# Fused FFT convolution and gated feed-forward: first filter spectrum from partial sums, short convolution on two halves of the array's rows, three weight groups kept from block to block, and a new order

## The chip, the cores and the metric

The kernel runs on one core of one Trainium2 chip. The metric is the device time of one execution in microseconds (us). A core has five engines that run side by side: PE (TensorE, matrix products; its weight loads are listed as PEld), DVE (VectorE), ACT (ScalarE), POOL (GpSimd) and SP (SyncE, which here only issues DMAs). PE writes into PSUM; ACT or DVE must copy ("evict") what it wrote to SBUF before the bank can be used again.

## The reference

All data are bfloat16, the sequence has S = 2048 steps and D = 640 channels, the feed-forward is F = 1728 wide.

```python
x = A_q
k_shift = sum over t in 0..3 of k_pad[:, t:t+S, :] * shift_k[:, 3 - t]      # causal, 4 taps per channel
kv = k_shift * v
y = irfft(rfft(kv, zero-padded to 2S) * rfft(ssm_k, zero-padded to 2S))[:S] # long causal convolution per channel
y = y + kv * ssm_D
h = x + layernorm(x) * y
out = h + (silu(layernorm(h) @ w_gate) * (layernorm(h) @ w_up)) @ w_down
```

## The kernel before

The sequence is worked in four blocks j of 512 steps. A block is a tile of 128 partitions with R = 4 rows (r) of 640 channels each.

For every block, g (the filter `ssm_k`) is turned by PE transposes or by DMA (`g_turned`, L453). k goes through the 4-tap short convolution and is multiplied by v (`kv_of`, L621). `spectrum` and `transform` (L506, L369) turn g into G[j] and kv into X[j] by matrix products with a fixed cosine and sine basis WF (the helper `forward`, L375). The outputs come as two halves, "low" and "high", each with four rows of 640. By the rule "sub" the even rows r are summed first (evicted, times two), then the odd ones are added, and DVE takes the difference (L410). By `DIRECT`, which the first filter block G0 alone uses, the second half comes instead from two more products per group with a second basis, `minus` (L1205 loads it): 6 products of 320 columns where "sub" needs 4.

`window` joins two blocks' filter spectra to H. `mac` (L707) forms the products X[i]·H[j-i] and sums them into A on DVE: a term is a product (L746) and a sum (L747). The inverse (L813, matrix products L878 with WI), two layer norms (`norm`, L760, on DVE or POOL) and a turn of the result (`turn_h`) give hT. Some sums are handed to the DMA engines, which add into memory (`add_into`, L276); these are issued by POOL.

`ffn` (L966 on) takes block j - 1 while block j is transformed: seven weight groups of gate and up columns, each loaded by two (the last by four) DMAs (`load_w`, L959), 27 times 5 products of 512 columns (L1022), then 112 products of 320 columns (or as many columns cut otherwise) with w_down (L1110). All seven groups are loaded again in each of the four blocks. Only blocks 0 to 2 have a transform of another block beside them; the last block's feed-forward stands alone at the end.

The short convolution of block 0 (`mm`, L639) uses, for each r, 5 channel groups times 4 taps = 20 products of 128 columns: the stationary operand is a 128 by 128 piece of turned k, the moving one a diagonal matrix of that tap's weights (`diag`, filled at L1166). In blocks 1 to 3 (`mm2`, L648) two taps share one product: the tile T holds k twice, the second copy one step later on the other 64 partitions, so that a product over 128 partitions does two taps for 64 channels, with 64 columns; 20 products again. The copies inside T are made by DMA (L563) and by ACT (L565, `TCOPY`), and `pairs` is a second table of tap weights (L1185, on POOL, from a second turn of the taps at L1175).

The order of all work is written out by hand, not found at build time: each piece of work is an `Op` with a number, and `ORDER` lists these numbers. An entry -n takes the piece's second form (`op.other`, another engine or queue). Every engine runs its own pieces in the order of the list and waits, in order, for what they need. Tiles named big, S, row, ps and so on are buffers out of pools (12 big, 8 S, 5 row, 4 ps); which one a piece gets follows from `ORDER` too.

```python
op = self.ops[n if n >= 0 else ~n]
...
if n < 0:
    op.eng, op.ns, op.fn = op.other
```

The first lines of the program keep PE busy with products of ones (`spin`, L1151, 18, 16 and 16 of them).

Of the kernel before, what the change touches and what calls it, by code (L numbers as in the profile page):

```python
# [31 lines left out]
ADDLO = ('G1', 'G2', 'X1', 'X2', 'X3')  # L32
ADDMAC = ()
ADDWIN = (1,)
ADDH = (1, 2)
LEAD = {}
PAD = 16
DIRECT = ('G0',)
ACTLN = 0
ACTKV = 0  # L40
ACTLN2 = (0, 1, 2, 3)
LN1DVE = ()
LN2POOL = (1, 2)
HTURN = (1, 3, 2)
GTURN = (3,)
KTURN = (1, 2, 3)
SUM = {'X3': 'four', 'i2': 'four', 'i3': 'four', 'G3': 'four'}
ADDP = {(1, 1): ((0, 1),)}
ADDINV = (2,)
WHOLE3 = False  # L50
WARMUP = (18, 16, 16)
MERGE = ()
WIDE = ()
H1ACT = ()
PAIRED = True
K0TURN = False
EARLY = True
FFN4 = True
KVPAIR = ()
DPOOL = False  # L60
LASTCUT = 2
DIAGDVE = 4
ATURN = ()
GLOAD = (1, 2, 3, 'T')
FIRST = False
TWOTAPS = True
TWONS = 640
TCOPY = (1, 2)
# [43 lines left out]
HALVES = (ROWS[:2], ROWS[2:])  # L112


def make_basis():

# [96 lines left out]
def kernel(ctx: ExitStack, tc: tile.TileContext, A_q, A_k, A_v, A_shift_k, A_ssm_k, A_ssm_D, B_x,  # L213
# [369 lines left out]
    def load_k(j):  # L583
        if TWOTAPS and j:
            return load_two(j)
# [745 lines left out]
```

## Time and profile before

| | |
|---|---|
| time, median of 3 runs (lowest to highest) | 261.48 us (260.77 to 261.54) |
| the profiled execution's own time: span, first to last instruction | 259.6 us |
| PE busy | 251.3 us (97%) |
| DVE busy | 198.6 us (77%) |
| ACT busy | 180.0 us (69%) |
| POOL busy | 97.0 us (37%) |
| moved by DMA | 45.38 MB |
| granted TensorE clock | 1.000 |

The profiled execution has only its span; the runs' median lies 1.9 us above it. "Busy" of PE counts a product from its start to its modelled end, and products overlap, so PE's rate is read from the spacing of a run of products, not from its busy time. A line number is a line of the kernel before; in the kernel after the same statement has another number, and the table of the change gives those that matter.

### The profile page before, as it was taken

What the parts mean: (1) busy time and instruction counts of PE and PEld (TensorE: products, weight loads), DVE (VectorE), ACT (ScalarE), POOL (GpSimd) and SP (SyncE); (2) the same over time, 40 slices, a digit from 0 to 9 for tenths busy, and PEclk for the clock granted to TensorE, in tenths of its full rate; (3) what the DMA queues carried; (4) which work ended last, traced back from release to release, by engine and by line L of the source; (5) the groups of instructions that cost most, each with busy time, mean ns of one, the idle gap of its engine ahead of it and who ended that gap; (6) DMA issues with size and microseconds to landing.
All of it is one profiled execution on the core that took longest, in us unless ns stands there. A gap on an engine that the chain in (4) does not pass through costs nothing.

```text
span 259.6 us, 4700 instructions
## 1 busy us (share of the span) xinstructions
PE 251.3 (97%) x1803; PEld 154.2 (59%) x1818; DVE 198.6 (77%) x259; ACT 180.0 (69%) x297; POOL 97.0 (37%) x115
## 2 busy tenths in 40 slices
PE   8999899999998999999999999999999999999994
PEld 7967577654654477754465477544456764444663
DVE  4679999999998999999999999999998200004403
ACT  2899999999998998569855985655497134637200
POOL 7961300008914199926117962240951022000000
PEclk9999999999999999999999999999999999999999
DMA  6997999979999998999997965994498546000002
GB/s 218 403 251 119 289 252 340 280 115 279 247 238 168 182 217 204 190 191 201 214 231 110 299 151 107 198 238 130 100 215 255 101 77 70 8 0 0 13 15 76
DMA packets 64752, 45.38 MB, mean 175 GB/s; under 512 B 31014, under 2 KB 60267, under 8 KB 64731
## 3 DMA queue, kind: packets, MB, share of 16 engines
q1 hardware_dynamic: 58896, 32.96, 51.1%
q0 software_dynamic: 5824, 12.13, 24.9%
q8 instruction: 14, 0.23, 0.4%
q14 instruction: 8, 0.06, 0.1%
q10 hardware_dynamic: 10, 0.01, 0.0%
HBM read 30.01 MB, written 4.59 MB: 133 GB/s over the span
## 4 chain that ended last, share of the span: by engine, by line
PE 78%; ACT 9%; DMA 6%; DVE 2%; issue 2%; SPq 1%; ACTq 0%; DVEq 0%
PE ps L1022 40%; PE ps L1110 23%; PE ps L375 10%; DMA big<-in_B_w_up_dram 4%; PE ps L878 3%; DMA big<-in_A_q_dram 3%; ACT T L565 2%; ACT big L364 1%; ACT S L364 1%; PE ps L648 1%; ACT row L757 1%; ACT big L664 1%; ACT big L473 1%; ACT tT L1014 1%; DVE row L892 1%
## 5 line engine op out<-in xcount | busy, mean ns | idle before, releaser
L1022 PE MATMUL ps<-big,big 128*128 128x512 bf16 x525 | 119.9, 379 | 1.7 <-DMA big<-in_B_w_up_dram 0.8
L1022 PEld LDWEIGHTS <-big 128*128 128x128 bf16 x540 | 52.5, 98 | 61.1 <-DMA big<-in_B_w_up_dram 1.3
L1110 PE MATMUL ps<-wd,tT 128*128 128x320 bf16 (+1 forms) x416 | 60.3, 299 | 0.0
L1110 PEld LDWEIGHTS <-tT 128*128 128x128 bf16 x416 | 40.7, 98 | 16.3
L1016 DVE TENSOR_TENSOR tT<-tT,co 128x2048 bf16<-128x2048 bf16 x12 | 14.5, 1219 | 34.4 <-ACT tT L1014 32.4
L375 PE MATMUL ps<-big,WF 128*128 128x320 bf16 x240 | 39.1, 299 | 1.3 <-ACT big L364 1.0
L1012 ACT CAST co<-ps 128x1024 bf16<-128x1024 f32 x24 | 24.2, 1011 | 17.3 <-PE ps L1022 16.8
L747 DVE TENSOR_TENSOR S<-S,big 128x2560 bf16<-128x2560 bf16 x23 | 34.3, 1492 | 1.2 <-DMA S<-big 0.5
L746 DVE TENSOR_TENSOR big<-S,S 128x2560 bf16<-128x2560 bf16 x23 | 34.1, 1485 | 0.2
L375 PEld LDWEIGHTS <-WF 128*128 128x128 bf16 x240 | 23.1, 97 | 12.8 <-issue 2.3
L1014 ACT ACTIVATE tT<-ps 128x1024 bf16<-128x1024 f32 x24 | 24.5, 1029 | 8.8 <-PE ps L1022 8.7
L757 ACT ACTIVATE row<-big 128x640 bf16<-128x640 bf16 x32 | 23.5, 742 | 1.8 <-DMA big<-in_A_q_dram 1.1
L807 ACT ACTIVATE row<-big,sm 128x640 bf16<-128x640 bf16 x23 | 20.3, 922 | 3.8 <-POOL sm L789 2.8
L1117 POOL DMA_DIRECT2D out_dram<-row x12 | 11.8, 1010 | 29.2 <-ACT row L1116 29.1
L364 ACT CAST S<-ps 128x320 bf16<-128x320 f32 (+1 forms) x36 | 19.4, 583 | 0.3
L1116 ACT CAST row<-ps 128x640 bf16<-128x640 f32 x12 | 8.1, 691 | 14.2 <-PE ps L1110 13.2
L364 ACT ACTIVATE big<-ps 128x640 bf16<-128x640 f32 (+1 forms) x24 | 15.6, 696 | 0.7 <-PE ps L375 0.7
L278 POOL DMA_DIRECT2D big<-row x8 | 7.0, 919 | 22.9 <-DVE row L892 22.9
L892 DVE SCALAR_TENSOR_TENSOR row<-row,ps 128x640 bf16<-128x640 bf16 x16 | 12.8, 815 | 1.1 <-PE ps L878 0.9
L278 POOL DMA_DIRECT2D S<-big x2 | 2.5, 1266 | 26.3 <-DVE S L719 19.1
L719 DVE TENSOR_TENSOR big<-S,S 128x2560 bf16<-128x2560 bf16 (+1 forms) x10 | 12.2, 1218 | 0.1
L959 POOL DMA_DIRECT2D big<-in_B_w_gate_dram x8 | 9.1, 1137 | 8.1 <-PE ps L1022 7.8
(110 smaller groups left out, 330.4 us busy)
## 6 DMA issues: line engine op xcount, KB each, us to landing
big<-in_B_w_up_dram SPq DMA_DIRECT2D x17, 320.0 KB, 5.1
big<-in_B_w_gate_dram SPq DMA_DIRECT2D x16, 320.0 KB, 4.7
big<-in_A_ssm_k_dram SPq DMA_DIRECT2D x4, 640.0 KB, 9.2
big<-in_A_q_dram SPq DMA_DIRECT2D x4, 640.0 KB, 7.6
big<-in_A_v_dram SPq DMA_DIRECT2D x4, 640.0 KB, 6.9
big<-in_B_w_gate_dram POOLq DMA_DIRECT2D x8, 320.0 KB, 7.2
big<-in_B_w_up_dram POOLq DMA_DIRECT2D x7, 320.0 KB, 6.7
wd<-in_B_w_down_dram SPq DMA_DIRECT2D x1, 2080.0 KB, 12.2
```

What stands on the lines that cost most here:

```text
L364: (lambda: nc.scalar.activation(dst(), src(), ACT.Copy, scale=2.0)) if twice else (lambda: nc.scalar.copy(dst(), src())),
L375: nc.tensor.matmul(ap(ps)[:, h, 0:NH], w, ap(src)[:, r, h * NH:(h + 1) * NH], start=(first and i == 0), stop=(last and i == len(rs) - 1), ...
L746: nc.vector.tensor_mul(flat2(b), X.part(xs), H.part(hs))
L747: f(A.part(dst), A.part(dst), flat2(b))
L757: act(825, lambda r=r, junk=junk: nc.scalar.activation(ap(junk), ap(x)[:, r, :], ACT.Square, scale=D ** -0.5, accum_out=sm(s, 1)[:, r:r + ...
L807: nc.scalar.activation(ap(row), ap(x)[:, r, :], ACT.Identity, bias=sm(s, 5)[:, r:r + 1], scale=sm(s, 4)[:, r:r + 1])
L892: nc.vector.scalar_tensor_tensor(two(ap(t)), two(ap(t)), 1.0, half(ap(ps)), op0=ALU.mult, op1=ALU.mult, accum_out=sm(s, 0)[:, r:r + 1])
L1012: act(1010, lambda ps=ps: nc.scalar.copy(ap(co)[:, at:at + 2, :], ap(ps)), src, [(co, gi % 2)])
L1014: act(1010, lambda ps=ps: nc.scalar.activation(ap(tT)[:, c:c + 2, :], ap(ps), ACT.Silu), src, [done(range(c, c + 2), ROWS)])
L1016: dve(1220, lambda: nc.vector.tensor_mul(ap(tT)[:, c - 2:c + 2, :], ap(tT)[:, c - 2:c + 2, :], ap(co)), [co], [done(range(c - 2, c + 2), R ...
L1022: nc.tensor.matmul(ap(ps)[:, i, :], ap(w)[:, k, off:off + P], ap(hT)[:, k, :], start=(k == 0), stop=(k == KT - 1))
L1110: nc.tensor.matmul(ap(ps)[:, hf, to:to + n], t, ap(wd)[:, c, col + (hf - hs[0]) * NH:col + (hf - hs[0]) * NH + n], start=(c == order[0]), ...
```

## The change

It has five parts, made together.

1. G0 comes by "sub" like the other blocks (`DIRECT` is empty): 32 products of 320 columns in place of 48, the `minus` basis is not loaded, and DVE takes two differences of half width more.
2. The short convolution of every block uses one table `diag` (128 by 64 for a channel group and tap) and one copy of k. A product runs over 64 partitions, the lower or the upper half of the array's rows, with 64 columns; for each r there are 5 groups times 4 taps times 2 halves = 40 products, alternating between the halves, and the halves write to two PSUM banks. The second copy of k in T, `pairs`, the second turn of the taps and all copies inside T go. A small tile `halo` keeps the last three steps of block 0.
3. `load_w` keeps the last three weight groups of a block for the next one (`KEEP`), and every second block takes the groups in reversed order, so that the kept ones come first.
4. Every sum that may be made by DVE or by a DMA is now one helper (`sum_into`), and the choice is made by the sign in `ORDER`; likewise the layer norms (POOL or DVE). On DVE 17 of the sums at L622 (before L747: 23) are left; the DMA makes 10 sums of 640 KB (before 4) and 6 of 160 KB (before 8). Four norms run on DVE (before two).
5. `ORDER` is new throughout, and the third `spin` is gone.

| what | line before | line after |
|---|---|---|
| transform products | L375 | L353 |
| short convolution | L639, L648 | L577 |
| tap table | L1166, L1185 | L965 |
| inverse products | L878 | L748 |
| gate and up, down | L1022, L1110 | L852, L906 |
| product, sum of a term | L746, L747 | L619, L622 |
| weight loads | L959 | L810 |

```diff
-DIRECT = ('G0',)
+DIRECT = ()
-WARMUP = (18, 16, 16)
+WARMUP = (18, 16)
-GLOAD = (1, 2, 3, 'T')
+GLOAD = (0, 1, 2, 3)
+KEEP = (3, 3, 3)
-    0, 2, 31, 1, 4, 5, 7, 10, 6, 8, 16, 13, 12, 11, 22, 29, 26, 37, 27, 14, 3, 15, 23, 28, 42, -39, 9, 35, -37, 24, 39, 205, 40,
+    4, 0, 21, 2, 14, 1, 3, 5, 20, 7, 6, 46, 18, -48, 48, 50, 8, 51, 52, 24, -54, 19, 22, 49, -14, 30, -26, 54, 28, 26, 31,
...
+GROUPS = (0, 1, 2, 3, 4, 5, 6)
...
-    def add_into(to, what, r, w, n=R * D):
+    def sum_into(ns, fn, to, what, r, w, n=R * D, dma=False):
+        def by_dma():
+            nc.gpsimd.dma_start(out=to(), in_=what(), accum_op=ALU.add, max_dma_last_dim=2 * D * 2)
+        a, b = ("dve", ns, fn), ("add", 958.0 if n == D else 3830.0, by_dma)
...
+    T = fixed([P, KT * TW], BF16, "T")
+    halo = fixed([P, KT, 3], BF16, "halo")
+    diag = fixed([P, KT, 4, H2], BF16, "diag")
...
-            def mm(r=r, ps=ps):
+            def mm(r=r, out=out):
                 for c in range(KT):
                     for t in range(4):
-                        q, off = (r - t, PAD) if r >= t else (r - t + 4, PAD - 1)
-                        k = tk0()[:, c, q, off - PAD + 1:off - PAD + 1 + P] if TWOTAPS else ap(kT)[:, c, q, off:off + P]
-                        nc.tensor.matmul(line(ap(ps))[:, c * P:(c + 1) * P], k,
-                                         ap(diag)[:, 4 * c + t, :], start=(t == 0), stop=(t == 3))
+                        for b in range(2):
+                            at = slice(b * H2, (b + 1) * H2)
+                            if j:
+                                k = tk()[at, c, PAD + r - t:PAD + r - t + 4 * P - 3:4]
+                            else:
+                                q, off = (r - t, 1) if r >= t else (r - t + 4, 0)
+                                k = tk0()[at, c, q, off:off + P]
+                            nc.tensor.matmul(out()[:, b, c, :], k, ap(diag)[at, c, t, :], start=(t == 0), stop=(t == 3))
...
-            def mm2(r=r, ps=ps):
-                for c in range(KT):
-                    for b in range(2):
-                        lo = c * P + b * H2
-                        for p in range(2):
-                            at = PAD + r - 2 * p
-                            nc.tensor.matmul(line(ap(ps))[:, lo:lo + H2], tk()[:, b, c, at:at + 4 * P - 3:4],
-                                             ap(pairs)[:, 4 * c + 2 * b + p, :], start=(p == 0), stop=(p == 1))
...
     def load_w(gi):
+        if gi in kept:
+            return kept[gi]
...
+        kept[gi] = w
+        return w
...
+        order = GROUPS if j % 2 == 0 else GROUPS[::-1]
+        for n, gi in enumerate(order):
...
+            if j == NB - 1 or n < NGRP - KEEP[j]:
+                kept.pop(gi)
```

How the order moves, at three places. First SP's queue at the start: the loads of block 0 (ssm_k is g, q is x). Before:

```order
L597 DMA T<-in_A_k_dram 128x2560
L330 DMA big_73<-in_A_ssm_k_dram 128x5x512
L342 DMA big_74<-in_A_q_dram 128x2560
L337 DMA big_75<-in_A_v_dram 128x2560
L1199 DMA WF<-const_wf 128x2048
L342 DMA big_76<-in_A_q_dram 128x2560
L1205 DMA tT_84<-const_minus 128x2048
```

and now:

```order
L308 DMA big_72<-in_A_ssm_k_dram 128x5x512
L514 DMA big_73<-in_A_k_dram 128x2560
L977 DMA WF<-const_wf 128x2048
L320 DMA big_75<-in_A_q_dram 128x2560
L315 DMA big_76<-in_A_v_dram 128x2560
L308 DMA big_79<-in_A_ssm_k_dram 128x5x512
```

The filter and the basis WF moved ahead of k and of x and v; `minus` is gone.

Second, POOL at the start, where the tap table is filled. Before, `big_72` holds diag (DVE fills the other 16 pieces):

```order
L1180 TENSOR_TENSOR row_87<-ident 128x64
L1170 COPY row_87<-row_86 5x512
L1166 TENSOR_SCALAR big_72<-ident,taps 128x128 x4
L1188 MEMSET root 128x4
L1189 MEMSET tail 64x512
L1185 TENSOR_SCALAR pairs<-row_87,taps_107 128x64 x12
```

and now:

```order
L960 TENSOR_TENSOR row_86<-ident 128x64
L986 DMA row_87<-in_A_ssm_D_dram 1x16x40
L965 TENSOR_SCALAR diag<-row_86,taps 128x64 x8
L547 COPY halo<-T 128x15
L965 TENSOR_SCALAR diag<-row_86,taps 128x64 x4
L969 MEMSET root 128x4
```

POOL now fills 12 of the 20 pieces that the first convolution reads, and the last four stand behind a copy that reads all of block 0's turned k.

Third, POOL a little later, while block 1 is transformed: the sums that DMAs make (S is a spectrum, `sm` the small tile of a layer norm). Before:

```order
L554 COPY T<-T 64x10x3
L278 DMA S_71<-big_75 128x2x1280
L775 TENSOR_TENSOR sm_98<-sm_98 128x4
L785 TENSOR_TENSOR sm_98<-sm_98 128x4
L786 TENSOR_SCALAR sm_98<-sm_98 128x4
L787 TENSOR_TENSOR sm_98<-sm_98,root 128x4
L789 TENSOR_TENSOR sm_98<-sm_98 128x4
L278 DMA S_67<-S_69 128x2x1280
```

and now:

```order
L255 DMA S_67<-S_68 128x2x1280
L255 DMA S_71<-big_72 128x2x1280
L653 TENSOR_TENSOR sm_99<-sm_99 128x4
L663 TENSOR_TENSOR sm_99<-sm_99 128x4
L664 TENSOR_SCALAR sm_99<-sm_99 128x4
L665 TENSOR_TENSOR sm_99<-sm_99,root 128x4
L666 TENSOR_TENSOR sm_99<-sm_99 128x4
L255 DMA S_71<-S_71 128x2x1280
```

Before, these were two of the four sums of 640 KB in the whole queue; now they are the first three of ten, and a window sum stands ahead of the norm.

More of the change, by code (lines that the diff above doesn't have):

```diff
@@ L600, in turned_k @@
     def turned_k(k, behind=None, table=None):
-        if plan.block in KTURN or not plan.block and K0TURN:
+        if plan.block:
             return k
-        src = rd if plan.block else plain
-        kT = T if TWOTAPS else new("kT")
         for r in range(R):
@@ L614, in turned_k @@
             evict(lambda copy, r=r, pt=pt: copy(
-                tk0()[:, :, r, 1:] if TWOTAPS else ap(kT)[:, :, r, PAD:], turned(pt)[:, 0:D].rearrange("p (c t) -> p c t", c=KT)),
-                [pt], [of_t(("K", r)) if TWOTAPS else (kT, r)], other=490)
+                tk0()[:, :, r, 1:], turned(pt)[:, 0:D].rearrange("p (c t) -> p c t", c=KT)), [pt], [of_t(("K", r))], other=490)
             if table:
                 plan.ops[-1].deps.add(table)
-        return kT
-    def kv_of(j, kT, before, v, behind=None):
-        two_taps = TWOTAPS and j > 0
-        if j == 0:
-            dve(60, lambda: nc.vector.memset(tk0()[:, :, :, 0:1] if TWOTAPS else ap(kT)[:, :, :, PAD - 1:PAD], 0.0), [],
-                [of_t("K0") if TWOTAPS else (kT, "halo")])
-        elif not two_taps:
-            plan.add("pool", 900, lambda: nc.gpsimd.tensor_copy(ap(kT)[:, :, :, PAD - 1:PAD], ap(before)[:, :, :, PAD + P - 1:]),
-                     [(before, r) for r in range(R)], [(kT, "halo")])
+        firsts.append(plan.add("pool", 500, lambda: nc.gpsimd.tensor_copy(ap(halo), tk0()[:, :, 1:R, P]), [of_t(*FIRSTS)], [halo], (),
+                               ("act", 240, lambda: nc.scalar.copy(ap(halo), tk0()[:, :, 1:R, P]))))
@@ L630, in kv_of, with by_half, out @@
+        return T
+    firsts = []
+    def kv_of(j, v, behind=None):
+        if j == 0:
+            dve(60, lambda: nc.vector.memset(tk0()[:, :, :, 0:1], 0.0), [], [of_t("K0")])
         kv = new("t4")
-        for r in (0, 2, 1, 3) if plan.block in KVPAIR else range(R):
+        def by_half(t):
+            return t.rearrange("p (c b x) -> p b c x", c=KT, b=2)
+        for r in range(R):
             ps = conv_ps()
-            def mm(r=r, ps=ps):
+            def out(ps=ps):
+                return half(ap(ps)).rearrange("p b (c x) -> p b c x", c=KT)
+            def mm(r=r, out=out):
@@ L707, in mac, with straight @@
-    def mac(A, X, H, first, pieces=((0, 1),), adds=(), at=None):
-        if at in MERGE:
-            merged(A, X, H, first, [a for a in adds if isinstance(a, int)])
-            return
-        adds = [a for a in adds if not isinstance(a, int)]
+            if j == 0:
+                firsts.append(op)
+            def straight(r=r, out=out):
+                nc.vector.tensor_mul(by_half(ap(kv)[:, r, :]), out(), by_half(rd(v)[:, r, :]))
+            op = plan.add("act", 700, lambda r=r, out=out: nc.scalar.copy(by_half(ap(kv)[:, r, :]), out()), [ps, v], [(kv, r)], (), ("dve", 820, straight))
@@ L714, in mac @@
+            op.rest = dve(490, lambda r=r: nc.vector.tensor_mul(ap(kv)[:, r, :], ap(kv)[:, r, :], rd(v)[:, r, :]), [v], [(kv, r)])
+        return kv
+    def mac(A, X, H, first, pieces=((0, 1),)):
         for ws in pieces if first else ():
@@ L961, in load_w, with ffn @@
         plan.name = was
-        return (w, 0), (w, 2 * P)
-    paired = []
-    def ffn(j, hT, h, end=False, lead=0):
+        kept[gi] = w
+        return w
+    kept = {}
+    def ffn(j, hT, h, end=False):
         tT = new("tT")
@@ L1080, in ffn @@
-        first, then = ROWS[:2], ROWS[2:]
-        for gi in range(0, lead, 2):
-            chunks((gi, gi + 1), first)
-        for gi in range(lead, NGRP - 1):
-            by_four(gi) if FFN4 else chunks((gi,), ROWS)
-        behind = odd_by_four() if FFN4 else odd_chunks()
-        for gi in range(0, lead, 2):
-            behind = chunks((gi, gi + 1), then)
+        order = GROUPS if j % 2 == 0 else GROUPS[::-1]
+        for n, gi in enumerate(order):
+            if gi == NGRP - 1:
+                last = odd_by_four()
+            else:
+                close = gi // 2 in [g // 2 for g in order[:n]]
+                if not close:
+                    co = new("co")
+                last = by_four(gi, co, close)
+            if j == NB - 1 or n < NGRP - KEEP[j]:
+                kept.pop(gi)
@@ L1088, in ffn @@
+        behind = last
         for r in ROWS:
             ps = new("ps_f")
-            order = list(range(lead * 2, NCH)) + list(range(lead * 2))
+            order = list(range(NCH))
             last = end and r == ROWS[-1]
@@ L1190 @@
     plan.add("pool", 600, lambda: nc.gpsimd.memset(ap(wd)[64:P, NC_FULL, :], 0.0), [ident], [(wd, "zero")])
-    turns = [op for op in plan.ops if op.eng in ("turn", "aturn")]
     first("Lx0")
     x = load_x(0)
-    if FIRST:
-        plan.ops[-1].then.update(turns)
     first("Lv0")
@@ L1202 @@
     first("Lm")
-    minus = new("tT")
+    minus = new("tT") if DIRECT else None
     if DIRECT:
@@ L1212 @@
     first("k0")
-    k = turned_k(k, spun, table)
-    again = spun
-    if not K0TURN:
-        again = spin(WARMUP[2])
-        again.deps.update(op for op in plan.ops if op.name == "k0" and op.eng == "pe" and op is not again)
-    kv = kv_of(0, k, None, v, again)
+    turned_k(k, spun, table)
+    kv = kv_of(0, v)
     first("g0")
@@ L1229 @@
     A = Spec(new("S"))
-    at = len(plan.ops)
     mac(A, X[0], H[0], True, split("m"))
-    plan.ops[at].then.update(fills)
     first("i0")
-    s = inverse(A, x, n1, split("i"), minus if "inv0" in DIRECT else None, HALVES if LEAD.get(0) else (ROWS,))
+    s = inverse(A, x, n1, split("i"), minus if "inv0" in DIRECT else None, (ROWS,))
     first("t0")
@@ L1248 @@
         stage("Lk")
-        before, k = k, load_k(j)
+        load_k(j)
         stage("Lv")
```

402 lines of the change are left out of this document (91 added, 311 removed), and 72 rows, old and new, of the table ORDER.

## The prediction

> **What bounds the kernel now.** I read the page's busy times first, then the busy time by stretch, then the chain of waits, and last the timelines of the places that the change touches. The page's first row says that PE is busy almost throughout; the table by stretch (PE, DVE and ACT, each with its time and its count of instructions) says where each engine is.
>
> ```profile
> PE 251.3 (97%) x1803; PEld 154.2 (59%) x1818; DVE 198.6 (77%) x259; ACT 180.0 (69%) x297; POOL 97.0 (37%) x115
> ...
> 12.80:28.00 15.20, 14.57 (x116) 10.10 (x114) 13.31 (x24) 14.83 (x42) 5.85 (x14) 1.00 0.97 196
> 28.00:50.00 22.00, 20.50 (x223) 15.02 (x222) 21.55 (x44) 21.49 (x40) 2.44 (x4) 1.00 1.11 286
> 50.00:82.00 32.00, 30.90 (x225) 16.80 (x228) 31.42 (x31) 30.78 (x42) 14.46 (x12) 1.00 0.99 225
> 82.00:197.00 115.00, 114.58 (x723) 66.30 (x730) 112.59 (x108) 85.46 (x136) 59.62 (x56) 1.00 0.88 189
> 212.00:256.00 44.00, 43.90 (x243) 23.82 (x244) 7.28 (x9) 15.92 (x19) 2.58 (x3) 1.00 0.13 21
> ```
>
> Up to 197 us two engines are full at once, PE and DVE (112.59 of 115 us); after 212 us PE is alone. PE busy can hide a slow stream, so I check its rate in the chain of waits (start, length, what).
>
> ```profile
> 97.53 2.72 PE ps L1110 x20
> ...
> 114.09 10.74 PE ps L1022 x49
> ...
> 130.01 0.66 PE ps L648 x20
> ...
> 189.99 0.54 PE ps L878 x4
> ```
>
> A product of 320 columns takes 2.72/20 = 136 ns, one of 512 columns 219 ns, one of 64 columns 33 ns; from 81 us to the end the chain is PE products one behind the other. So PE's count of products times these spacings is the span, plus the head, the tail and the gaps. The gaps behind the head are small: 0.63 + 1.50 + 1.10 us in the first three stretches, 0.42 us in the fourth. DVE nevertheless sets PE at one late place, the inverse of block 3:
>
> ```profile
> 186.62 1.49 DVE L826 TENSOR_TENSOR S<-S 128x2560 bf16<-128x2560 bf16 x1
> 188.14 1.56 DVE L843 TENSOR_TENSOR S<-S 128x1280 bf16<-128x1280 bf16 x2
> ```
>
> L843 ends at 189.70 us and its reader L878 starts at 189.99 us. A saving on PE ahead of that place needs a saving on DVE as well, or other work for PE to do meanwhile.
>
> **First G.** 48 products become 32; 16 fewer at 136 ns are **-2.2 us** on PE, all on the path, since the stretch is PE and evictions wall to wall. Their loads go with them, so `minus` is not missed. DVE gets two half-width differences, counted below.
>
> **Short convolution, block 0.** PE at the head, before:
>
> ```profile
> 4.92 0.68 PE L610 MATMUL ps<-ident,T 128*128 128x128 bf16 x5
> 5.53 0.25 PE L1175 MATMUL ps<-ident,row 5*128 5x5 bf16 x4
> 5.71 1.01 PE L610 MATMUL ps<-ident,T 128*128 128x128 bf16 x15
> 6.56 1.10 PE L1151 MATMUL ps<-const-bfloat16-1.0 128*128 128x128 bf16 x16
> 7.50 1.00 PE L471 MATMUL ps<-ident,big 128*128 128x128 bf16 x15
> 8.34 4.63 PE L639 MATMUL ps<-big,T 128*128 128x128 bf16 x80
> 12.80 1.04 PE L375 MATMUL ps<-big,WF 128*128 128x320 bf16 x6
> ...
> L610 PE MATMUL ps<-ident,T 128*128 128x128 bf16 x20 | 1.7, 240 | 0.0
> ...
> L1175 PE MATMUL ps<-ident,row 5*128 5x5 bf16 x4 | 0.2, 164 | 0.0
> ```
>
> The 80 products run from 8.34 to 12.80 us: 4.46 us. What 40 half-row products take is in no row of before. If the two halves run side by side, 20 pairs of 64 columns cost what the 20 products of L648 cost, 0.66 us for an r; nothing is gained on that by either half being narrower. The columns alone give (219 - 136)/192 = 0.43 ns each, so 64 columns could come to 29 ns and the r to 0.59 us. If every product starts only when the one before it has left, the nearest row is L1175: four products of 5 columns in 0.25 us, of which the last takes 0.164, so 29 ns from start to start: 40 of them are 1.15 us. I take 0.66 us, since its products have the same columns and the same weights to load, and keep 0.59 and 1.15. Block 0: 4 x 0.66 - 4.46 = **-1.8 us**; blocks 1 to 3: 12 x (0.66 - 0.66) = **0**. [...]
>
> **Passing from full rows to half rows.** L1175 uses only a part of the rows, and PE goes into it and out of it. The five products before it have a spacing of (0.68 - 0.24)/4 = 0.11 us, still the slow pace of the start; the last of them began at 4.92 + 0.68 - 0.24 = 5.36 us, and L1175 0.17 us later: 0.06 extra, or 0.115 against the pace of L639, 4.46/80 = 0.056. On the way back 5.71 - 5.53 = 0.18 us hold four spacings of 29 ns and 0.064 extra. I take 0.12 us for a trip. PE's order after the change has 12 runs of half-row products, so **+1.4 us**, with 0 and 12 x 0.18 = 2.2 as bounds.
>
> **The head.** What the first products wait for, in this program's own loads (KB each, us from issue to landing):
>
> ```profile
> T<-in_A_k_dram SPq DMA_DIRECT2D x1, 640.0 KB, 3.9
> ...
> 1.72 7.11 DMA big<-in_A_q_dram
> ...
> L1185 POOL TENSOR_SCALAR pairs<-row,taps 128x64 bf16<-128x64 bf16 x20 | 9.3, 487 | 0.1
> ...
> L1166 DVE TENSOR_SCALAR big<-ident,taps 128x128 bf16<-128x128 bf16 x16 | 3.0, 319 | 0.1
> ...
> L614 DVE COPY T<-ps 128x640 bf16<-128x640 bf16 x2 | 0.9, 470 | 0.0
> ...
> L477 DVE TENSOR_TENSOR big<-big,row 1x640 bf16<-1x640 bf16 x1 | 0.5, 490 | 0.0
> ...
> L550 POOL COPY T<-T 64x15 bf16<-64x15 bf16 x1 | 0.4, 367 | 0.0
> ```
>
> The first load of 640 KB, issued at 0.8 us, lands at 4.7; the third lands at 8.8, so one takes 2.1 us. Now g lands first, at about 4.9, k at 6.9, WF (512 KB) at 8.5. PE turns g (20 products, 1.1 us) by 6.0, waits for k, turns it by 8.0, waits for WF and does 22 products of G0 (3.0 us) until 11.5. The sixteen products of ones that went are no gain by themselves: they ended at 7.5, when the next load was there. All this leaves the head **+0.2 us** against the same work before.
>
> Then the first convolution needs all of diag. POOL fills 8 pieces of 128 by 64, copies the halo, which waits for all four evictions of turned k and for DVE's memset behind its own 8 fills, and fills 4 more. On DVE two evictions of turned k and the D row (0.47 to 0.49 us each) run from about 7.3 to 8.7, its 8 fills, at half the 3.0/16 us of before, to 9.5, an eviction and the memset to 10.1; then 0.37 + 4 x 0.49 us on POOL end at 12.4 us. PE is there at 11.5, so **+1.0 us** with rounding up, between 0 (if the fills keep pace) and 2.5.
>
> **Freed engines.** ACT loses three copies of 2.33 us, DMA 2 x 3 copies of 320 KB, and 7 of the 24 pairs of weight loads.
>
> ```profile
> L565 ACT COPY T<-T 64x2570 bf16<-64x2570 bf16 x3 | 6.9, 2330 | 1.2 <-DMA T<-T 1.2
> L747 DVE TENSOR_TENSOR S<-S,big 128x2560 bf16<-128x2560 bf16 x23 | 34.3, 1492 | 1.2 <-DMA S<-big 0.5
> L410 DVE TENSOR_TENSOR S<-big,S 128x1280 bf16<-128x1280 bf16 x2 | 1.7, 826 | 1.1 <-ACT S L364 1.1
> L778 DVE TENSOR_SCALAR sm<-sm 128x4 int32<-128x4 int32 x2 | 0.3, 170 | 0.1
> ...
> 81.11 1.25 PE L1022 MATMUL ps<-big,big 128*128 128x512 bf16 x4 [0.78 <-DMA big<-in_B_w_up_dram]
> ```
>
> On DVE 6 sums of 1.49 us go (-8.9), two half differences come (+1.7), two norms of ten small operations at 0.17 us come (+3.4), and the fills are half as many and half as wide (3.0 to about 0.8: -2.2), together some -6 us, all ahead of block 3's inverse. So the place at 189.7 us moves at least as much as PE does, and PE's saving is not lost there. Of the 3.2 us of gaps behind the head I take **-0.9 us**: 0.78 of them was a weight load that came late, and fewer loads share the queues, but the buffers that hold kept weights are missing elsewhere. Bounds: -2.5 and +0.5.
>
> **Sum.** -2.2 - 1.8 + 1.4 + 0.2 + 1.0 - 0.9 = -2.3 us on the profiled span of 259.6, so 257.3; the profiled span lies 1.9 us under the median, and the median falls alike: 261.5 - 2.3 = **259.2 us**. With the low ends (0.59 us for each r: -1.1; no trips: -1.4; gaps -2.5: -1.6; not all at once) it goes to about 256.5, with the high ends, the convolution apart, to about 262.5.
>
> **Rivals.** (1) The halves do not run side by side. Every half-row product then starts 29 ns behind the one before: 16 x (1.15 - 0.66) = +7.8 us on top of the forecast, 267.0 us. It decides from a spacing of 20 ns, where 16 x 40 x (20.1 - 16.5) ns = 2.3 us undo the gain. For it: the only small products in the trace keep 29 ns. Against it: those share one part of the rows, these alternate. [...] Chance 0.15.
>
> (2) Sums by DMA come late. There are ten of 640 KB where there were four:
>
> ```profile
> S<-big POOLq DMA_DIRECT2D x2, 640.0 KB, 8.3
> S<-S POOLq DMA_DIRECT2D x2, 640.0 KB, 8.8
> ```
>
> Sums into the same A follow one another, and each lands 8.3 us after its issue against 1.49 on DVE. Two such places late by 1.5 us each on DVE cost 3.0 us where PE has no other work in its order: 262.2 us. Against it: 0.5 us of DVE idle in the row L747 above is all that four sums cost before. Chance 0.17.
>
> (3) No change: the head's wait for diag and the trips at their high ends (+1.5, +0.8) and no gap closed (+0.9) give 262.4 at worst, about 261.5 if two of them hold. Chance 0.13.
>
> **How the numbers follow.** The forecast has 0.55, its own range 256.5 to 262.0. About 0.3% (0.8 us) is what a measurement of this kernel can tell from no change, so faster means under 260.7. Faster: 0.48 of the forecast's 0.55, and 0.03 each of rivals 2 and 3: 0.54. Same: 0.05, 0.04 and 0.06: 0.15. Slower: all of rival 1, 0.15, and 0.10, 0.04 and 0.02 of the others: 0.31. The range 256.5 to 264.5 leaves out rival 1 and 0.03 below.
>
> **What would show it.** Half-row products: 40 in 0.66 us on PE's timeline (right), over 0.9 us (rival 1). G0: 32 products. PE's idle time ahead of the first convolution: about 1.0 us, ended by POOL. Gaps of some 0.12 us around each of 12 runs. DVE busy near 193 us, and block 3's inverse read by PE at about 187 us; a longer idle time of DVE at the sums, ended by DMA, is rival 2. The prediction is wrong in its working if the time falls while these rows do not.

## The result, and the profile after

The kernel after takes **277.92 us** (median of 4 runs, 275.25 to 279.20); the kernel before, beside it, 261.12 us (260.46 to 261.54). The ratio is 1.063, with a 95% interval of 1.057 to 1.070. The forecast was 259.2 us, between 256.5 and 264.5: wrong in sign. The profiled execution of the kernel after took 275.25 us with a span of 273.5 us and a granted clock of 0.981, so it is 13.9 us longer than the profiled span of before. Below, a ratio leaves out every run that is over 1.5% above the fastest of its kernel, and a median takes all runs, so the two need not agree.

The page's first row of the kernel after:

```profile
PE 252.1 (92%) x2087; PEld 150.6 (55%) x2102; DVE 192.2 (70%) x270; ACT 172.6 (63%) x292; POOL 100.1 (37%) x91
```

And its waits of PE (who waited, for what: us in total, times, longest):

```profile
PE ps L852 <- ACT co L841: 5.7, 1, 5.7
PE ps L577 <- issue: 3.2, 2, 2.0
PE ps L852 <- ACT tT L843: 2.0, 1, 2.0
PE ps L437 <- DMA big<-in_A_ssm_k_dram: 1.9, 2, 1.1
PE ps L748 <- DVE row L762: 1.2, 1, 1.2
```

PE's busy time is as before (251.3), in a longer span: 14 us of waits in five rows. It holds two stretches at half clock, 3.4 us from 35.3 us on and 6.8 us from 144.5 us on. The largest wait looks like ACT's doing, so I follow ACT at that place (start, length, what; in brackets the idle time before, and what ended it):

```profile
135.48 1.02 ACT L843 ACTIVATE tT<-ps 128x1024 bf16<-128x1024 f32 x1 [0.49 <-PE ps L852]
141.77 0.92 ACT L684 ACTIVATE row<-big,sm 128x640 bf16<-128x640 bf16 x1 [5.26 <-POOL sm L666]
145.60 0.92 ACT L684 ACTIVATE row<-big,sm 128x640 bf16<-128x640 bf16 x1 [2.91 <-DMA out_dram<-row]
146.42 0.99 ACT L841 CAST co<-ps 128x1024 bf16<-128x1024 f32 x1
```

ACT takes its operations in the order of the program: L841 starts at 146.42 us, behind both L684, though PE's last product ahead of its pause ended at 141.73. It stands at L684, which applies the layer norm, first because the norm (`sm`) is not there, then because an output transfer, which POOL issues behind the norm, has not freed a row. Behind it stands L841, the eviction that PE needs. So POOL is where the time starts. Its timeline, at the norms of blocks 1 and 2:

```profile
67.26 13.95 POOL L653 TENSOR_TENSOR sm<-sm 128x4 f32<-128x4 f32 x1 [2.35 <-ACT row L673]
81.28 0.20 POOL L663 TENSOR_TENSOR sm<-sm 128x4 f32<-128x4 f32 x1
...
119.80 19.92 POOL L653 TENSOR_TENSOR sm<-sm 128x4 f32<-128x4 f32 x1 [3.55 <-ACT row L673]
139.80 0.20 POOL L663 TENSOR_TENSOR sm<-sm 128x4 f32<-128x4 f32 x1
...
142.05 0.95 POOL L913 DMA_DIRECT2D out_dram<-row  x1 [0.32 <-issue]
142.71 1.24 POOL L810 DMA_DIRECT2D big<-in_B_w_up_dram  x1
```

One operation on 128 by 4 numbers lasts 13.95 and 19.92 us; the next of the same kind 0.20 us. Output and weight loads queue behind it. The same operation before, early and at block 1's norm:

```profile
15.63 0.20 POOL L775 TENSOR_TENSOR sm<-sm 128x4 f32<-128x4 f32 x1 [1.45 <-ACT row L796]
...
60.29 2.87 POOL L775 TENSOR_TENSOR sm<-sm 128x4 f32<-128x4 f32 x1
63.24 1.45 POOL L785 TENSOR_TENSOR sm<-sm 128x4 f32<-128x4 f32 x1
```

And DVE meanwhile, before:

```profile
60.22 1.48 DVE L410 TENSOR_TENSOR S<-big,S 128x2560 bf16<-128x2560 bf16 x1
61.62 1.48 DVE L746 TENSOR_TENSOR big<-S,S 128x2560 bf16<-128x2560 bf16 x1
63.14 1.49 DVE L747 TENSOR_TENSOR S<-S,big 128x2560 bf16<-128x2560 bf16 x1
64.55 1.48 DVE L746 TENSOR_TENSOR big<-S,S 128x2560 bf16<-128x2560 bf16 x1
```

DVE after:

```profile
68.91 2.88 DVE L619 TENSOR_TENSOR big<-S,S 128x2560 bf16<-128x2560 bf16 x2
71.72 4.29 DVE L622 TENSOR_TENSOR S<-S,big 128x2560 bf16<-128x2560 bf16 x3
...
80.67 0.48 DVE L587 TENSOR_TENSOR big<-big,big 128x640 bf16<-128x640 bf16 x1
```

Before, a sum (L747) stood right behind the product that it reads: 61.62 + 1.48 = 63.10, and the sum starts at 63.14, a pause of 0.04 us. POOL's operation ends there, at 63.16. After the change products and sums stand apart, and no operation needs the one just ahead of it: three sums take 4.29 us, so they start 1.40 us apart and last 1.49; each starts before the last one has ended. From 67 to 81 us DVE never pauses, and L653 ends at 81.21, when L587 (80.67 + 0.48 = 81.15) leaves the first pause. That is theory A: POOL gets in only where DVE pauses. The traces bear it out for the first operation of these two norms, not for all that follow: before, the next one, L785, ended at 64.69 us, where L747 (until 64.63) and the next product (from 64.55) overlap and there is no pause.

A second, smaller loss lies in the first 40 us. Pieces of the chain of waits of the kernel after:

```profile
12.18 1.27 PE ps L577 x80
...
30.16 2.06 PE ps L577 x107
32.22 1.97 issue
34.19 0.33 PE ps L577 x7
```

The stretch behind it in the table by stretch (last three columns: granted clock, DMA share, GB/s), after:

```profile
36.00:40.00 4.00, 4.00 (x30) 2.50 (x26) 1.19 (x3) 2.02 (x4) 1.42 (x3) 0.66 0.52 120
```

and before:

```profile
36.00:40.00 4.00, 3.79 (x75) 3.28 (x73) 3.93 (x10) 3.86 (x10) 0.17 (x1) 1.00 1.09 321
```

80 half-row products take 1.27 us, near the forecast of 2 x 0.66. But within such a run PE stops for 1.97 us, waiting for nothing that the profile shows ("issue"), and from 36 to 40 us the granted clock is 0.66.

### The profile page after: what moved, and what is told of

Its sections match the earlier page's. It is cut to its first block, busy times and chain, and to the rows that moved or that the text cites. A ratio compares the mean times of both kernels' runs of the same rounds, so it can differ in the third digit from the quotient of the medians.

```text
span 273.5 us, 5202 instructions
## 1 busy us (share of the span) xinstructions
PE 252.1 (92%) x2087; PEld 150.6 (55%) x2102; DVE 192.2 (70%) x270; ACT 172.6 (63%) x292; POOL 100.1 (37%) x91
## 4 chain that ended last, share of the span: by engine, by line
PE 60%; POOL 14%; ACT 9%; DMA 8%; issue 4%; DVE 2%; SPq 2%; POOLq 0%; ACTq 0%; DVEq 0%
PE ps L852 28%; PE ps L906 19%; POOL sm L653 12%; PE ps L353 6%; PE ps L577 3%; PE ps L748 3%; DMA big<-in_A_k_dram 2%; DMA big<-in_B_w_gate_dram 2%; DMA big<-in_A_ssm_k_dram 2%; ACT row L635 2%; DMA big<-row 2%; ACT S L342 2%; ACT big L342 1%; SPq L523 1%; ACT row L684 1%
## 5 line engine op out<-in xcount | busy, mean ns | idle before, releaser
L852 PE MATMUL ps<-big,big 128*128 128x512 bf16 x525 | 119.5, 383 | 9.3 <-ACT co L841 5.7
L852 PEld LDWEIGHTS <-big 128*128 128x128 bf16 x540 | 52.7, 98 | 71.5 <-issue 9.9
L906 PE MATMUL ps<-wd,tT 128*128 128x320 bf16 (+2 forms) x416 | 60.1, 299 | 0.8 <-DVE row L923 0.6
L906 PEld LDWEIGHTS <-tT 128*128 128x128 bf16 x416 | 40.6, 98 | 17.2 <-issue 0.8
L653 POOL TENSOR_TENSOR sm<-sm 128x4 f32<-128x4 f32 x4 | 35.8, 8959 | 10.5 <-ACT row L673 10.5
L353 PE MATMUL ps<-big,WF 128*128 128x320 bf16 x240 | 38.9, 303 | 0.6 <-ACT big L439 0.2
L841 ACT CAST co<-ps 128x1024 bf16<-128x1024 f32 x24 | 24.1, 1012 | 22.8 <-PE ps L852 22.3
L846 DVE TENSOR_TENSOR tT<-tT,co 128x2048 bf16<-128x2048 bf16 x12 | 14.5, 1219 | 33.9 <-ACT tT L843 26.1
L619 DVE TENSOR_TENSOR big<-S,S 128x2560 bf16<-128x2560 bf16 x24 | 35.1, 1485 | 0.0
L353 PEld LDWEIGHTS <-WF 128*128 128x128 bf16 x240 | 23.1, 99 | 13.5 <-issue 3.4
L684 ACT ACTIVATE row<-big,sm 128x640 bf16<-128x640 bf16 x22 | 19.5, 917 | 12.9 <-POOL sm L666 9.2
L255 POOL DMA_DIRECT2D S<-big x8 | 10.8, 1351 | 42.5 <-DVE big L619 14.3
L622 DVE TENSOR_TENSOR S<-S,big 128x2560 bf16<-128x2560 bf16 x17 | 24.9, 1486 | 0.0
L342 ACT ACTIVATE big<-ps 128x640 bf16<-128x640 f32 (+1 forms) x32 | 18.3, 622 | 3.8 <-PE ps L353 3.8
L342 ACT CAST S<-ps 128x640 bf16<-128x640 f32 (+1 forms) x28 | 16.0, 623 | 1.7 <-PE ps L353 1.7
L577 PE MATMUL ps<-diag,T 64*128 64x64 bf16 x640 | 13.3, 196 | 3.3 <-issue 3.2
L577 PEld LDWEIGHTS <-T 64*128 64x128 bf16 x640 | 11.9, 111 | 5.2 <-issue 4.7
```

The lines of the kernel that those rows point to most:

```text
L342: (lambda: nc.scalar.activation(dst(), src(), ACT.Copy, scale=2.0)) if twice else (lambda: nc.scalar.copy(dst(), src())),
L353: nc.tensor.matmul(ap(ps)[:, h, 0:NH], w, ap(src)[:, r, h * NH:(h + 1) * NH], start=(first and i == 0), stop=(last and i == len(rs) - 1), ...
L577: nc.tensor.matmul(out()[:, b, c, :], k, ap(diag)[at, c, t, :], start=(t == 0), stop=(t == 3))
L619: dve(1490, lambda b=b, xs=xs, hs=hs: nc.vector.tensor_mul(flat2(b), X.part(xs), H.part(hs)), [X.at(xs), H.at(hs)], [b], [A.b])
L622: f(A.part(dst), A.part(dst), flat2(b))
L653: v.tensor_mul(sm(s, 6), sm(s, 2), sm(s, 2))
```

## The experiments

**Norms on DVE, and 15 memsets.** Two ways of taking away what theory A names. The first has POOL's two norms done by DVE:

```diff
-  433, 333, 273, 436,
+  433, 333, -274, 436,
...
-  631, 484, 535,
+  631, -485, 535,
```

> The first layer norms of blocks 1 and 2 move from POOL to DVE (9 small operations each); nothing else changes. Theory A: POOL's small operations on the norm are shut out as long as DVE runs one operation into the next, which is what cost 13.95 and 19.92 us at L653. Then the two waits vanish, DVE pays about 1.5 us for each norm, the PE gaps at 83, 86 and 141 us (1.4, 2.2, 5.9 us in the after trace) and the low clock behind the last one go: 264 to 269 us, and no POOL operation of 10 us is left. Rival B: POOL is held up by its own queue of DMA sums, and PE would have waited for late sums and weights anyway: 274 us or more. Rival C: the norms are a symptom and PE's gaps come from buffers of the new order: also 274 or more, with gaps in the same places.

The second leaves every instruction in its place, and puts a memset that nothing reads behind 15 of DVE's operations:

```diff
+    for _ in range(15):
+        dve(60, lambda: nc.vector.memset(ap(free), 0.0), [], [free])
-  259, 256, 261,
+  259, 256, 898, 261, 899,
```

> The norms stay on POOL and every instruction keeps its order; DVE gets 15 extra memsets of 128x4 (7 behind operations of the stretch 67 to 76 us, 8 in the stretch 120 to 130 us), which read nothing. Theory A: each is a place where POOL's next operation can get in, so L653 falls from 13.95 and 19.92 us to about 1 to 3 us each, the five operations of a norm take 4 to 8 us, and the time falls to 265 to 270 us although DVE has about 1.5 us more to do. Rival B (POOL's own DMA queue) and rival C: L653 stays above 10 us at both places and the time stays at 277 to 280 us. If L653 gets no shorter although the memsets stand there, what lets POOL in is a true pause of DVE and not an operation that reads nothing.

Measured: 263.36 us (262.98 to 265.35) and 263.74 us (263.65 to 263.95), each 1.011 of before (1.006 to 1.017 and 1.008 to 1.015). With the memsets, POOL:

```profile
67.46 1.80 POOL L653 TENSOR_TENSOR sm<-sm 128x4 f32<-128x4 f32 x1 [2.35 <-ACT row L673]
...
116.40 3.58 POOL L653 TENSOR_TENSOR sm<-sm 128x4 f32<-128x4 f32 x1 [3.54 <-ACT row L673]
```

and DVE:

```profile
67.71 1.49 DVE L598 TENSOR_TENSOR S<-S,big 128x2560 bf16<-128x2560 bf16 x1
69.12 1.49 DVE L619 TENSOR_TENSOR big<-S,S 128x2560 bf16<-128x2560 bf16 x1
69.15 0.06 DVE L1065 MEMSET free<- 128x4 f32 x1
70.54 1.49 DVE L619 TENSOR_TENSOR big<-S,S 128x2560 bf16<-128x2560 bf16 x1
```

The operations of 13.95 and 19.92 us take 1.80 and 3.58; the first ended at 69.26 us, right behind the first memset (69.15 to 69.21). The times are somewhat below what theory A gave: a memset costs DVE not 0.1 us but the step from 1.40 to 1.41 us between starts, 0.01 us. So 15 of them, 0.2 us of DVE, are worth 14 us: theory A is shown, for the norms of blocks 1 and 2, and PE's waits for ACT went with them. That also speaks against rivals B and C: the sums stayed in POOL's queue and the new order stayed as it was.

**Without the DMA sums ahead of the norms.** `-259, -462, -464, -472` become `258, 461, 463, 471` in the order of the kernel after.

> The four sums of 640 KB that POOL issues between 60 and 120 us (one just ahead of the norm of block 1, three ahead of the norm of block 2) go back to DVE; the norms stay on POOL. Rival B (POOL waits for its own DMA sums): L653 falls to under 3 us at both places and the time to 265 to 270 us. Theory A: DVE is no less dense, L653 stays above 8 us at both places unless a sum behind its own product happens to leave a pause, and the time is 275 to 284 us (DVE has 6 us more to do).

Measured: 275.53 us, one execution.

```profile
115.93 23.38 POOL L653 TENSOR_TENSOR sm<-sm 128x4 f32<-128x4 f32 x1 [13.99 <-ACT row L673]
```

Three sums fewer in POOL's queue, and the operation of block 2 is longer: rival B is out. At block 1 it fell to 1.23 us (66.21 to 67.43). The returned sum is not the reason; DVE happened to stand idle there, waiting for PE:

```profile
65.89 1.49 DVE L598 TENSOR_TENSOR S<-S,big 128x2560 bf16<-128x2560 bf16 x1
67.72 1.49 DVE L619 TENSOR_TENSOR big<-S,S 128x2560 bf16<-128x2560 bf16 x1 [0.34 <-PE ps L852]
```

**The other way round, in the kernel before.** In one term, sums stand one product late:

```diff
             def go(...):
                 nc.vector.tensor_mul(flat2(b), X.part(xs), H.part(hs))
-                f(A.part(dst), A.part(dst), flat2(b))
+                if was:
+                    was[1](A.part(was[2]), A.part(was[2]), flat2(was[0]))
+                if at != (1, 1) or (xs, hs) == (1, 0):
+                    f(A.part(dst), A.part(dst), flat2(b))
```

> The kernel before, with one change: in the second term of block 1, three products and their sums on DVE are written product, product, sum, product, sum, sum, so that no sum stands right behind its own product; same operations, same engines. Theory A: the short pauses behind a product at 62.8, 65.7 and 68.6 us disappear, the first POOL operation of the norm (2.87 us before) lasts until DVE next pauses, 8 us or more, PE waits, and the time rises by 2 to 10 us (263 to 271). Rival B or C: the operation stays at about 2.9 us, and the time within 0.5% of the kernel before.

Measured: 261.69 us, ratio 1.002 (0.999 to 1.005). In this kernel L747 is a product, L749 a sum and L782 POOL's first operation of the norm. POOL:

```profile
60.58 5.67 POOL L782 TENSOR_TENSOR sm<-sm 128x4 f32<-128x4 f32 x1
```

and DVE:

```profile
64.71 1.49 DVE L749 TENSOR_TENSOR S<-S,big 128x2560 bf16<-128x2560 bf16 x1
66.23 1.49 DVE L747 TENSOR_TENSOR big<-S,S 128x2560 bf16<-128x2560 bf16 x1
```

The operation grew from 2.87 to 5.67 us and ended at 66.25, at the first pause that was left (64.71 + 1.49 = 66.20, next start 66.23). I had counted on no pause before 68 us, so 8 us was too much, and the time was the same: DVE waited until 69.97 us for a DMA sum anyway. That supports the mechanism, but the forecast of a longer time failed: a delay of 3 us there cost nothing.

**What is left: PE out of code?** With the norms mended the kernel is 1.1% slower than before, not faster. Three kernels, all with the norms on DVE. The first issues the load of w_down (2080 KB) later:

```diff
-  74, 203, 186, 211,
+  74, 203, 211,
...
-  171, 194, -325,
+  171, 194, 186, -325,
```

> The kernel with both norms on DVE (263.4 us), and on SP's queue the load of w_down (2080 KB, issued at 24.4 us, landed at 36.6) now stands behind the load of x of block 1 (about 44 us). What is left open there: PE stands still for 2.3 us at 31.9 us in the middle of the half-row products, with nothing that it waits for, and runs at half clock for 3.4 us from 35.5 on. Theory F: PE has run out of instructions; the next piece of its code (16 KB on the instruction queue) is fetched from 31.8 us on and comes late because the data transfers keep the DMA engines full. Then with 2 MB less in the way the pause falls under 1 us, the clock stays full, and the time is 259.5 to 261.5 us. Theory S: the fetch starts when PE has used up the code, whatever the DMA engines do: pause and clock stay, 262.5 to 264.5 us. Theory P: PE waits for a PSUM bank or for T: the same as S.

The second pulls the runs of block 1 apart (PE's order is 225, 207, 228, 209, 231, 406, 222 where it was 225, 228, 231, 207, 222, 406):

> The kernel with both norms on DVE (263.4 us); in block 1 the four runs of 40 half-row products no longer stand three in a row: groups of four filter products of 320 columns stand between them, and the evictions move with them. The same instructions, so PE needs about 1.1 us more to get through the code up to the place of the pause, and makes two more trips between full and half rows (2 x 0.3 us). Theory F or S (PE out of code): the pause of 2.3 us falls to 1.3 us or less, and the half clock behind it goes or shrinks: 261 to 263 us. Theory P (a buffer): a pause of over 2 us stands at the start of a run of products, with a wait: 263 to 265 us.

The third has `WARMUP = (18, 6)` in place of `(18, 16)`. Its norms too are on DVE, which its expectation does not say.

> The kernel after with 10 fewer products of ones at the start (20 PE instructions fewer), nothing else. In it PE paused behind its instructions number 449 and 961, which is 512 apart, or two pieces of 16 KB at 64 bytes an instruction. Theory F or S: the pauses stand behind the same numbers, so 10 products later: the first in the same run of half-row products but 10 products on, the second behind the third run and no longer in it. Theory P: they stand ahead of the same products as before (numbers 429 and 941). The time says little here, 275 to 280 us, since the norms are as in the kernel after.

Measured: 262.97 us (259.62 to 267.21), ratio 0.999 (0.996 to 1.003); 263.30 us (262.06 to 268.17), ratio 1.006 (1.004 to 1.008); 265.58 us, one execution. The first's ratio is of five of its ten runs; by its median it is 0.7% longer than before. PE in the third:

```profile
32.43 2.20 PE L577 MATMUL ps<-diag,T 64*128 64x64 bf16 x120
34.56 0.45 PE L353 MATMUL ps<-big,WF 128*128 128x320 bf16 x2
37.61 0.43 PE L353 MATMUL ps<-big,WF 128*128 128x320 bf16 x2 [2.60 <-issue]
37.98 0.86 PE L577 MATMUL ps<-diag,T 64*128 64x64 bf16 x40
```

and in the first:

```profile
31.26 2.21 PE L577 MATMUL ps<-diag,T 64*128 64x64 bf16 x120
33.40 0.72 PE L353 MATMUL ps<-big,WF 128*128 128x320 bf16 x4
```

In the kernel after, the pause came behind the 112th of 120 half-row products; with 10 products fewer at the start it comes behind all 120 and two products of 320 columns, exactly 10 products later. Counted in the trace's PE records, it stands behind instruction 961 in both, the earlier pause behind 449 in both, and 961 - 449 = 512. PE lacks instructions, not data: theory P is out. The records of the instruction queue have a piece of 16 KB starting at 31.8 us in the kernel after, 0.4 us before PE stops, and at 29.8 in the kernel with w_down later, although PE begins these runs 1.1 us later there (31.26 after 30.16); the pause is gone and the clock stays at 1.00 in this stretch: theory F is supported against S. The spread runs moved the pauses elsewhere: that kernel waits 1.6 us for transposes of k and 1.4 us for an eviction instead, and its ratio of 1.006 is no clear gain on 1.011 (1.006 to 1.017).

The page of the kernel after counts 16 pieces, 0.26 MB, on the instruction queue beside 4189 records of PE (2087 products, 2102 weight loads), that of before 14 pieces, 0.23 MB, beside 3621 (1803 and 1818). An estimate from these is 62 to 64 bytes an instruction, so that 16 KB hold some 260 and the 512 are about two pieces. Only two of the 16 pieces go with a pause of PE of over 1 us that the profile puts down to no wait, of 1.22 and 1.97 us; in the third kernel one is 2.60 us. A run of 40 half-row products is 80 instructions of PE, products and weight loads, in 0.64 us, where before it was 40 in 0.66.

**Both together.** Memsets, and w_down later:

> The kernel after with the 15 memsets on DVE (263.7 us) and the load of w_down behind that of x of block 1. If both causes are right and independent, POOL's operations stay at 1 to 4 us and the pause of 2.3 us inside the half-row products of block 1 is gone with the half clock behind it: 258.5 to 261.5 us. If the load of w_down only pushes its 12 us of transfer onto the weights of the first feed-forward, the time stays at 262.5 to 264.

The same with `WARMUP = (18, 24)`:

> The one before with 8 more products of ones in the second group (24 instead of 16), which fills the wait of about 1 us ahead of the first g product. Theory: in the runs on the second chip PE came to full pace only at 9.6 us instead of 5.9 us because it stood idle there, and the first filter spectrum began at 9.9 instead of 8.6 us; with the gap filled it begins at 8.6 to 8.9 us, so 0 to 1.3 us less than the one before: 257.5 to 260.5 us. Rival: PE's slow start has another cause: the time of the one before within 0.4 us.

The same with loads 193 and 390 swapped, and 396 behind 392:

> The one before, and on SP's queue g of block 2 and v of block 1 change places (g of block 2 now about 17 us earlier), and v of block 2 goes behind the transposes of k of block 2. Theory: PE waits 1.1 to 1.5 us for g of block 2 at 25.5 us; that wait goes, and nothing else is late: 0.8 to 1.5 us less than the one before, 256.5 to 259.5 us. Rival: v of block 1, which now lands at 26 to 29 us, is late for the product with the convolved k of block 1 (about 31 us), or the instruction fetch at 13 to 15 us is no earlier and the pause there grows: no gain or a loss of up to 1 us.

Measured: 264.89 us (259.51 to 268.46), ratio 0.998 (0.995 to 1.001); 266.19 us (261.62 to 267.18); 264.00 us (261.71 to 265.62), ratio 1.010 (1.007 to 1.013). All three profiles lose time in a new place. PE's longest wait in the first:

```profile
PE ps L852 <- DMA big<-in_B_w_gate_dram: 4.0, 1, 4.0
```

and in the third:

```profile
PE ps L852 <- DMA big<-in_B_w_gate_dram: 3.6, 1, 3.6
```

At 57 to 58 us a weight group is late, and 3.4 us at half clock follow. By its ratio, of five of its twelve runs, the first is level with before, by its median 1.5% longer, and its profiled execution, of 266.11 us, is one of the longer ones; that of the third, 264.60 us, is near its median and has the same wait. In the two kernels after these, with w_down's 2 MB behind the weights, PE has no such wait: w_down got in the way of the weights. More warm-up shortened PE's wait ahead of the first g (0.66 us, then 0.29, then none), but G0 began at 9.04, 8.73 and again 9.04 us, so no earlier start is shown, nor that the wait makes PE's start slow; the swap took away PE's wait of about 0.9 us for g of block 2. Neither shows in these times.

So w_down went behind the weights, with the swap and without:

> The kernel with memsets, more warm-up and swapped loads, with the load of w_down moved once more, from 40 us to about 71 us, behind the weights of the first feed-forward. Its first reader is at 95 us and it needs 12 to 16 us. In the run with w_down at 40 us PE waited 3.8 us at 56.1 us for a weight group that landed late (60.4 us, 14.1 us after its issue), and ran at half clock for 3.4 us behind it. Theory: w_down's 2 MB were in the way; the wait and the half clock go: 264.6 - 3.8 - 1.7 = 259.1 us, between 258 and 260.5. Rival: the group is late because its buffer comes free late; then the wait stays, 262 to 265 us.

> The same without the swapped loads: g of block 2, v of block 1 and v of block 2 are loaded as in the kernel after. Theory: PE's wait of about 1.1 us for g of block 2 at 25 us comes back, all else as in the run beside it: 0.8 to 1.5 us more. Rival: the swap only moved the wait: within 0.4 us of it.

Measured: 260.72 us, ratio 0.999 (0.996 to 1.001), and 261.30 us, ratio 1.002 (0.999 to 1.005). No wait for w_gate is left, but PE now waited 2.0 and 1.8 us for an eviction at 80 us. The swap is worth 0.6 us by the medians, less than expected, and the two intervals overlap. Last, w_down in the lull that its own move had left, at 26 to 36 us; and the same without the memsets, that is, the kernel after with four loads moved and 8 more products of ones:

> The kernel with memsets, more warm-up and swapped loads, with the load of w_down now behind the first weight load (26 us), where the DMA engines were busy for only 0.18 to 0.30 of the time from 28 to 36 us in the run with it at 66 us. There PE waited 2.1 us at 79.4 us ahead of gate and up products. Theory: that wait and the earlier one at 57 us are w_down's transfer in the way of weights; in the lull it is in nobody's way: 260.7 - 2.1 = 258.6 us, between 257.8 and 259.8. Rival: it holds up the piece of code again that PE needs at 31 us, pause and half clock come back: 261 to 263 us; or the wait at 79.4 us belongs to buffers of the new order: 260.3 to 261.3.

> The one before without the 15 memsets, so the kernel after with nothing but loads moved and 8 more products of ones. If POOL's wait for a pause of DVE and the loads are two independent causes, the first operations of the norms of blocks 1 and 2 take 10 to 20 us again and the time is 13 to 16 us above the one before: 271 to 275 us. If the late code piece had set the two in step (the norms only met a dense stretch of DVE because PE was late), it is under 265 us.

Measured: **260.01 us (258.04 to 265.01), ratio 0.995 (0.991 to 0.999)**, and 270.28 us, ratio 1.038 (1.032 to 1.043). First row of the page with the memsets:

```profile
PE 250.6 (98%) x2110; PEld 151.0 (59%) x2110; DVE 192.0 (75%) x285; ACT 172.2 (67%) x292; POOL 79.5 (31%) x91
```

POOL without them:

```profile
63.30 1.22 POOL L653 TENSOR_TENSOR sm<-sm 128x4 f32<-128x4 f32 x1 [3.13 <-ACT row L673]
112.24 19.94 POOL L653 TENSOR_TENSOR sm<-sm 128x4 f32<-128x4 f32 x1 [3.54 <-ACT row L673]
```

The first beats the kernel after by 6%, and the kernel before by 1% at most: 0.5 us by the medians (260.55 us beside it). Its profiled span, 256.6 us, is of one of its shorter executions (258.36 us). w_down is issued at 26.1 us there, only 1.1 us later than in the kernel after, but the piece of code that came at 31.8 us now starts at 26.6, ahead of nearly all of w_down, and PE's pause at these runs is gone. The second kernel shows that POOL's wait at block 2 does not come from the late code: the operation takes 19.94 us again. At block 1 DVE waited 0.34 us for PE and let POOL in, so whether a norm meets a dense stretch also depends on when it comes; the time rose by 10 us over the kernel with memsets and not by the 13 to 16 expected.

## Why the prediction was wrong

By the ratios: 1.063 after, 1.011 with the memsets (5.2% or 13.6 us less: POOL shut out), 0.995 with the loads moved too (1.6% or 4 us less: late code, late loads and the half clock behind them, which no run separates). What is left, 0.5% or 1.3 us below before (0.4 to 2.3 us by the interval, 0.5 by the medians), stands where the forecast had 2.3 us less. So the rest of the sum is of the right sign but not confirmed in its size: 8 products of ones and four moved loads are in it too, and what those would do for the kernel before was not tried.

- **The step that failed** is the one from "DVE some -6 us, all ahead of block 3's inverse" to "PE's saving is not lost there", with the term of -0.9 us for gaps. DVE's sum was right (192.2 after 198.6), but I counted DVE's time and not its pauses. POOL, which I priced only at the head, lived in those pauses: the term was some +14 us, and late code and loads put some 4 us more into it. Its bounds, -2.5 and +0.5, held no such case, and no rival did. The rows of before had the sign: L775 takes 0.20 us at 15.63 us and 2.87 us at 60.29.
- **Rival 2** (sums by DMA late on POOL's queue) looked at the right queue for the wrong reason: taking the sums away helped nothing at block 2.
- **First G** was right: the row of L353 counts 240 products where L375 had 256, 16 fewer.
- **The convolution itself** was right: 1.27/2 = 0.64 us for an r, forecast 0.66; rival 1 (1.15 us) is out. Two halves are a pair in 1.27/40 = 32 ns, the way out to the next product included; in the first run of 80 they start 3 or 4 ns apart, and one pair starts mostly 25 or 26 ns behind the second product of the pair before. The low bound of 0.59 us does not follow from its own figure: 0.43 ns a column gives 28 ns for 64 columns, so 0.55 us. What I left out is that half-row products double the instructions: PE's code then came late (3.2 us of pauses) with half clock behind one of them.
- **Trips** between full and half rows cost more than forecast: by the records' starts 95 ns extra going in and 110 coming out, most alike, so 12 x 0.2 = 2.4 us against 1.4, and over the bound of 2.2.
- **The head** came out right for partly wrong reasons: the first convolution began at 12.18 us against 11.5 + 1.0; but PE did not wait for diag: the halo's copy ran at 9.35 us, ahead of DVE's memset (10.74), and POOL's last fill ended at 11.2 us. Instead G0's 22 products took 3.5 us instead of 3.0.

## What to carry to other kernels

Before packing one engine densely, look for an engine that lives in its pauses: here the sign was the same small operation at 0.20 us in one place and 2.87 us in another. The reorder that took DVE's pauses away held POOL up for 13.95 and 19.92 us, and in this in-order program all that queued behind it; a memset put in on purpose let it in for 0.01 us of DVE. And count instructions as well as time: here a run issued 80 in 0.64 us where it was 40 in 0.66, beside a load of 2080 KB, and the code itself came late, with 1.97 us of pause.

## What was not expected of the hardware

- POOL's operation L653 lasted through twelve DVE operations that began after it (13.95 us) and through seventeen (19.92 us), all TENSOR_TENSOR and each starting up to 0.09 us before the last one ended; pauses of 0.03 us, or a memset of 0.06 us, let it in. At these two norms POOL did not get in between operations that overlap. Elsewhere it did: L785 before, at 64.63 us, and the first operation of block 3 in the kernel with w_down behind the weights and no swap (0.25 us) and in the last kernel (0.32 us). What decides is open. While L653 stood, POOL's transfers behind it were not issued: the output transfer behind the norm of block 2 is issued at 142.05 us.
- PE paused for 1.2 to 2.6 us inside a stream of products with no wait, with its code late: in the kernel after 1.22 us behind instruction 449 and 1.97 us behind 961, 512 apart, with a piece of code starting 1.3 us ahead of the first pause (at 13.5 us) and 0.4 us ahead of the second (at 31.8 us).
- With pauses of PE of 1.97, 4.0 and 5.7 us came 3.4, 3.4 and 6.8 us at half clock: in the kernel after from 35.3 us, 1.1 us behind the end of the first, and from 144.5 us, within the last (141.73 to 147.47). With one of 2.0 us (at 86 us of the kernel after) and one of 2.6 us there was no half clock. What decides that is open.
